# Weight loads issued at two points of an iteration behind a VectorE write, and a later spread of global values

## Chip, cores and metric

The kernel runs on one core of one Trainium2 chip. The metric is device time in microseconds (us) for one execution, the median of several; the profile is one execution recorded by the hardware. TensorE does the matmuls and transposes, VectorE and ScalarE the elementwise work on its results, GpSimd copies inside SBUF, and SyncE issues nearly all transfers from HBM. Each engine works through its own list of instructions in order; they meet at semaphores.

## What is computed

Three layers in float32 on 2176 tokens of width 512 (4 batches, 8 heads of 64; 32 global and 512 local tokens per batch).

```
# attention: global tokens see all; local ones the global tokens and neighbours within 32
out_g = softmax(q_g @ [k_g, k_l].T / 8) @ [v_g, v_l]
out_l = softmax([q_l @ k_g.T, where(|i-j| <= 32, q_l @ k_l.T, -1e9)] / 8) @ [v_g, v_l]
x = concat(out_g, out_l) as (2176, 512)
# soft mixture: 8 experts with 4 slots each
logits = x @ phi
slot_in = softmax(logits, over tokens).T @ x
slot_out[e] = relu(slot_in[e] @ w1[e]) @ w2[e]      # 512 -> 1024 -> 512
x = softmax(logits, over slots) @ slot_out
# feed-forward
h = x @ w_in                                        # 512 -> 2048
out = (h - tanh(h)) @ w_out                         # 2048 -> 512
```

## The kernel before

The order of all work is written out by hand: what the Python code emits first stands first in the list of its engine. The part that matters here is the attention loop, `for it in range(NG + 1)` at line 664, with NG = 32: eight stages `s` (a batch and a half of its heads each) of four iterations `t`.

Iteration `it` does, on TensorE and in this order: the scores of group `it` (`local_scores`, line 248, in two halves `h2`, each followed on VectorE by masked maxima, line 254, and on ScalarE by the exponentials), the transposes of the probabilities of `it-1` (line 269), the product with values of `it-2` (`local_values`, line 281, and `global_values`, line 475), then pieces of other work: scores of the global tokens (line 430), transposes of finished rows (line 311), logits and sums of the mixture (lines 344, 392).

GpSimd prepares operands, all through the helper at line 210. `spread_q(it+1)` copies the queries of the next iteration into the layout that its scores read. `roll_k(it)` and `roll_v(it-2)` shift keys and values by a window. `spread_k(s+1)`, once a stage at t = 1, copies the global keys from the block `qg` into the key tile. `spread_v(s+1)`, once a stage at t = 3, copies the global values of `v[96:128, 0]` into the groups 1 to 5 of the same rows, so that every window's product also covers the global tokens. `local_values` of stage `s` begins in iteration 4s+2.

SyncE issues the loads, in the order in which the code emits them, all through `load` (line 98), which also adds their KB to `queued`. Per stage: queries every second iteration (256 KB, `load_q`), values at t = 2 and t = 3 (`load_v`), `qg` and keys of stage s+2 at the end of t = 3 (`load_qk`, 96 and 576 KB). Between them the loop at line 724 issues weights of later layers: one slot of 512 KB after another (`load_w`, or `load_raw` for the 64-bit words of `w_in`, two transfers of 256 KB), until `queued` reaches a target or slots run out:

```
while queued < LEAD + PACE * it:      # LEAD, PACE = 2700, 1200
```

There are 29 slots. A slot that has not been used has no earlier reader, so its load waits for nothing but its turn on SyncE. Raw words are converted during the loop (`win_head` on ScalarE, `win_ops` on VectorE), and their slots come back. What holds SyncE are the loads whose targets are still read: the queries wait for `spread_q`, `qg` and keys for the global and local scores.

After the loop (about 130 us) come the mixture, lines 971 and 1010, and from about 185 us the feed-forward with lines 1133 and 1174 to 1176.

Of the kernel before, what the change touches and what calls it, by code (L numbers as in the profile page):

```python
# [8 lines left out]
F32 = mybir.dt.float32  # L9
# [8 lines left out]
NST = 8  # L18
NT = 17
NE = 8  # L20
WARM = 3
LEAD, PACE = 2700, 1200
KEEP = 2
SPK = 1
C0 = 4
NIN = 8
# [36 lines left out]
def band_attention_soft_moe_tanhshrink_kernel(  # L63
# [15 lines left out]
    V, S, G, T, DMA = nc.vector, nc.scalar, nc.gpsimd, nc.tensor, nc.sync  # L79
# [47 lines left out]
    def spread_v(s):  # L127
        v = v_t[s][96:128]
        pcopy(v[:, 1:6], v[:, 0:1].to_broadcast([32, 5, 260]))
# [106 lines left out]
    def local_scores(g, fill):  # L236
        s, t = divmod(g, 4)
        k = k_t[s]
        sm = wk.tile([128, 512], F32, tag="sm", name="sm").rearrange("p (j c) -> p j c", j=4)
        mb = wk.tile([128, 4], F32, tag="mb", name="mb")  # L240
        for f in fill[0:1]:
            f()
        for h2 in range(2):
            sc = psS.tile([128, 2, 128], F32, tag="S", name="sc", padded_shape=[128, 2, 256])
            for a in range(2):
                jj = 2 * h2 + a
                for i in range(2):
                    T.matmul(  # L248
                        sc[64 * i:64 * i + 64, a, :], lhsT=q_b[2][:, 256 * i + jj:256 * i + 256:4],
                        rhs=k[:, i, :, WINDOWS[t][jj][0]], skip_group_check=True, tile_position=(0, 64 * i),  # L250
                    )
            for a in range(2):
                jj = 2 * h2 + a
                V.tensor_tensor_reduce(  # L254
                    out=sm[:, jj, :], in0=sc[:, a, :], in1=mask[WINDOWS[t][jj][1]],
                    scale=-0.125, scalar=3e38, op0=ALU.add, op1=ALU.min, accum_out=mb[:, jj:jj + 1],
                )
                S.activation(  # L258
                    out=sm[:, jj, :], in_=sm[:, jj, :], func=AF.Exp, scale=-1.0, bias=mb[:, jj:jj + 1]
                )  # L260
            for f in fill[1 + h2:2 + h2]:
                f()
        sm_t[g] = sm

    def local_transpose(g):
# [239 lines left out]
    free = [(wA, f"w{i}", 1024, 1) for i in range(NSLOT)]  # L505


    def slot(rounded=False):
        kinds = [tuple] if rounded else [(bass.AP, tuple)] if len(w_sl) < len(wq) else [bass.AP, tuple]
        if not any(isinstance(f, k) for k in kinds for f in free):  # L510
            free.extend(cool)
            cool.clear()
        src = free.pop(next(i for k in kinds for i, f in enumerate(free) if isinstance(f, k)))
        if not isinstance(src, tuple):
            return src, src
        pool, tag, width, bufs = src
        return pool.tile([128, width], F32, tag=tag, name="slot", bufs=bufs)[:, 0:1024], src


    def f64_words(src, room=None):  # L520
# [100 lines left out]
    def load_raw():  # L621
        c = len(raw_t)
        raw_t.append(f64_words(wind[:, c, :]))
# [16 lines left out]
    with tc.manual_schedule():  # L640
# [20 lines left out]
        load_v(1, 1)  # L661
        load(out=phi, in_=phid[0])
        fill = []
        for it in range(NG + 1):
            s, t = divmod(it, 4)
            open_chains()
# [42 lines left out]
                spread_k(s + 1)  # L709
            if it == 0:  # L710
                spread_v(0)
            if it < NG and t == 3 and s < NST - 1:
                spread_v(s + 1)
            if it % 2 == 0 and it < NG - 4:
                load_q(it // 2 + 2)
            if it < NG:
# [4 lines left out]
                if t in (2, 3) and 1 <= s < NST - 1:  # L721
                    load_v(s + 1, t - 2)

            while queued < LEAD + PACE * it:
                if len(raw_t) < min(NIN, (it - C0 + 3) // 2 + 1) and free:
                    load_raw()
                elif not len(free) > (KEEP if len(raw_t) < NIN else 0) or not load_w():
                    break
            if it < NG and t == 3 and s + 2 < NST:
                load_qk(s + 2)  # L730
            if it == NG - 5 or it == NG - 1:
# [772 lines left out]
```

## Time and profile before

| what | value |
|---|---|
| three timed runs | 403.26, 405.3, 407.09 us; median 405.3 |
| profiled execution | 406.85 us, of which the span from first to last instruction is 405.1 |
| TensorE clock granted | 0.993 of full speed over the span |
| TensorE matmul busy | 382.9 us, 95% |
| VectorE, ScalarE, GpSimd busy | 276.2, 218.2, 209.7 us |
| read from HBM | 65.22 MB, of 70.43 MB moved |

A stretch's busy time of one engine says how much of it the engine worked; the rest is idle time, and the views of waits say what ended it. The profile calls TensorE's matmuls PE and its loading of the stationary operand PEld, VectorE DVE, ScalarE ACT, GpSimd POOL, and the issuing part of SyncE SPq. "issue" as the cause of a wait means that the profile shows no releaser. A transfer has two times: when SyncE issued it, and how long after that it landed.

### The profile page before, as it was taken

To read this page: it belongs to the slowest core of one execution; us is meant where nothing else is said; L and a number is where in the kernel's file an instruction comes from. 1 tells how busy PE (TensorE), PEld (TensorE's weight loads), DVE (VectorE), ACT (ScalarE), POOL (GpSimd) and SP (SyncE) were. 2 spreads that over 40 slices of the span, in tenths; PEclk is the share of its full clock that TensorE was granted. 3 is DMA by queue.
4 is the path that set the end of the run, shared out by engine and by line. 5 is a ranking of instruction groups with operands and counts; after the bars stand their busy time and mean duration, and the time that the engine had idled before them with its cause. 6 is when DMAs were issued, how large, how long until landed. Compare 5 with 4: busy or idle time off the path is not lost.

```text
span 405.1 us, 10230 instructions
## 1 busy us (share of the span) xinstructions
PE 382.9 (95%) x3767; PEld 279.6 (69%) x3767; DVE 276.2 (68%) x833; ACT 218.2 (54%) x542; POOL 209.7 (52%) x275
## 2 busy tenths in 40 slices
PE   7889889989999899999999999999989999999994
PEld 3677667766787433336877786786868888888873
DVE  4577698766476526449998886787879997555541
ACT  2677666865766202248655645566575645345330
POOL 3676576665564010016866444455575668347441
PEclk9999999999999999999999999999999999999998
DMA  6899999999768989999303101003100003002104
GB/s 182 264 401 317 321 335 268 357 334 294 266 183 270 332 254 418 416 420 385 111 0 105 53 1 53 0 4 94 60 2 2 0 28 129 0 2 113 44 2 138
DMA packets 33834, 70.43 MB, mean 174 GB/s; under 512 B 3824, under 2 KB 10736, under 8 KB 33776
## 3 DMA queue, kind: packets, MB, share of 16 engines
q1 hardware_dynamic: 33632, 69.56, 50.3%
q8 instruction: 32, 0.52, 0.5%
q14 instruction: 26, 0.21, 0.2%
q10 hardware_dynamic: 144, 0.13, 0.1%
HBM read 65.22 MB, written 4.46 MB: 172 GB/s over the span
## 4 chain that ended last, share of the span: by engine, by line
PE 76%; issue 6%; POOL 5%; DVE 4%; DMA 3%; ACT 3%; SPq 2%; DVEq 0%; POOLq 0%
PE a L1175 13%; PE a L1176 13%; PE a L1174 13%; PE sc L248 7%; PE a L971 4%; PE a L1010 4%; PE h L1133 4%; PE X L281 3%; PE ptp L269 3%; SPq L104 2%; PE gsc L430 2%; POOL q L210 2%; PE xTp L311 2%; PE ps L344 1%; DVE slot L1150 1%
## 5 line engine op out<-in xcount | busy, mean ns | idle before, releaser
L1161 POOL TENSOR_TENSOR slot<-slot 128x384 fp32r<-128x384 f32 x96 | 98.7, 1031 | 83.5 <-ACT slot L1157 79.8
L1174 PE MATMUL a<-slot 128*128 128x512 f32 x272 | 106.9, 393 | 1.3 <-ACT v_w L1182 0.7
L1176 PE MATMUL a<-slot 128*128 128x512 f32 x272 | 107.8, 396 | 0.0
L1175 PE MATMUL a<-slot 128*128 128x512 f32 x272 | 107.5, 395 | 0.0
L1146 DVE SCALAR_TENSOR_TENSOR h<-slot,h 128x384 f32<-128x384 f32 x96 | 51.5, 537 | 38.7 <-ACT slot L1140 38.4
L1157 ACT CAST slot<-slot 128x384 fp32r<-128x384 f32 x96 | 47.6, 496 | 49.5 <-DVE slot L1150 49.0
L1140 ACT ACTIVATE slot<-h 128x384 f32<-128x384 f32 x96 | 45.3, 473 | 34.5 <-PE h L1133 33.9
L1174 PEld LDWEIGHTS a<-slot 128*128 128x128 f32 x272 | 51.1, 188 | 14.2 <-ACT v_w L1182 1.5
L1176 PEld LDWEIGHTS a<-slot 128*128 128x128 f32 x272 | 51.0, 188 | 11.4
L1175 PEld LDWEIGHTS a<-slot 128*128 128x128 f32 x272 | 51.0, 188 | 9.3 <-POOL slot L1037 1.0
L1150 DVE TENSOR_TENSOR slot<-slot,h 128x384 f32<-128x384 f32 x96 | 50.8, 529 | 8.0 <-DVE h L1146 0.5
L258 ACT ACTIVATE sm<-sm,mb 128x128 f32<-128x128 f32 x128 | 41.2, 396 | 15.5 <-DVE mb L254 15.2
L248 PE MATMUL sc<-k,q 128*64 128x128 f32 x512 | 39.0, 294 | 4.9 <-POOL q L210 3.8
L210 POOL TENSOR_SCALAR v<-v 32x1300 f32<-32x1300 f32 (+5 forms) x40 | 34.2, 855 | 13.9 <-PE xgp L475 11.4
L248 PEld LDWEIGHTS sc<-k,q 128*64 128x64 f32 x512 | 33.3, 208 | 11.1 <-POOL q L210 5.9
L210 POOL TENSOR_SCALAR q<-q 64x256 f32<-64x256 f32 x62 | 27.5, 444 | 20.5 <-issue 11.0
L254 DVE CUSTOM_DVE_ANT_0 sm<-sc,mask 128x128 f32<-128x128 f32 x128 | 30.2, 284 | 10.9 <-PE sc L248 9.7
L1037 POOL TENSOR_TENSOR slot<-k_w,slot 128x512 fp32r<-128x512 f32 x16 | 20.7, 1296 | 32.5 <-ACT slot L1036 32.3
L1133 PE MATMUL h<-slot 128*128 128x384 f32 x96 | 32.4, 339 | 0.8 <-DVE slot L1150 0.6
L1133 PEld LDWEIGHTS h<-slot 128*128 128x128 f32 x96 | 17.9, 188 | 12.0 <-DVE slot L1150 5.9
L281 PE MATMUL X<-v,pt 128*32 128x65 f32 x1024 | 22.1, 223 | 1.4 <-issue 1.4
L281 PEld LDWEIGHTS X<-v,pt 128*32 128x32 f32 x1024 | 16.5, 109 | 7.2 <-issue 6.1
(239 smaller groups left out, 526.2 us busy)
## 6 DMA issues: line engine op xcount, KB each, us to landing
slot<-in_w_dram SPq DMA_DIRECT2D x55, 512.0 KB, 7.6
slot<-in_w_out_dram SPq DMA_DIRECT2D x9, 512.0 KB, 4.8
slot<-in_w_in_dram SPq DMA_DIRECT2D x16, 256.0 KB, 6.5
k<-in_k_dram SPq DMA_DIRECT2D x7, 576.0 KB, 7.8
q<-in_q_dram SPq DMA_DIRECT2D x15, 256.0 KB, 5.4
out_dram<-o SPq DMA_DIRECT2D x15, 256.0 KB, 2.1
slot<-in_w_in_dram SPq DMA_DIRECT2D x7, 512.0 KB, 10.0
v<-in_v_dram SPq DMA_DIRECT2D x8, 390.0 KB, 5.5
```

What stands on the lines that cost most here:

```text
L210: G.tensor_scalar(out=o, in0=i, scalar1=0.0, scalar2=1.0, op0=ALU.add, op1=ALU.mult)
L248: T.matmul(sc[64 * i:64 * i + 64, a, :], lhsT=q_b[2][:, 256 * i + jj:256 * i + 256:4], rhs=k[:, i, :, WINDOWS[t][jj][0]], skip_group_check ...
L281: T.matmul(X[32 * jj:32 * jj + 32, h, :], lhsT=pt[:, 128 * jj + 32 * h:128 * jj + 32 * h + 32], rhs=v[:, WINDOWS[t][jj][0], 65 * h:65 * h ...
L1133: T.matmul(h, lhsT=mst(128 * fc, 128), rhs=cst(128 * t0 + c.start, n))
L1140: S.activation(out=u, in_=h, func=AF.Square)
L1146: V.scalar_tensor_tensor(out=h, in0=u, scalar=-2.5, in1=h, op0=ALU.add, op1=ALU.mult)
L1150: V.tensor_tensor(out=g, in0=u, in1=h, op=ALU.mult)
L1157: S.copy(out=ghi, in_=g)
L1161: G.tensor_tensor(out=glo, in0=g, in1=ghi.bitcast(F32), op=ALU.subtract)
L1174: T.matmul(acc_t[j], lhsT=ghi[:, c], rhs=whi[fc], start=first, stop=False)
L1175: T.matmul(acc_t[j], lhsT=ghi[:, c], rhs=wlo[fc], start=False, stop=False)
L1176: T.matmul(acc_t[j], lhsT=glo[:, c], rhs=whi[fc], start=False, stop=last)
```

## The change

The body of the loop at line 724 becomes a function `load_ahead(it, to)`. It is called at the end of an iteration, as before, and for iterations 2 to 26 also in the middle of `local_scores`, after VectorE's masked maxima of the first half, with half an iteration less in the target. LEAD grows from 2700 to 3300. In these iterations the first slot taken in each call is written by VectorE, one element, before its load is issued, so that the load waits for VectorE to have come to that point of its list; later loads stand behind it on SyncE. The spread of global values of stage `s` (from the second stage on) is emitted at the end of iteration 4s+1 instead of 4s-1; at t = 1 it follows `spread_k` on GpSimd.

```
-LEAD, PACE = 2700, 1200
+LEAD, PACE = 3300, 1200
@@ local_scores, at the end of each half h2
+            if h2 == 0 and 2 <= g < NG - 5:
+                load_ahead(g, g - 0.5)
@@ slot
-        return pool.tile([128, width], F32, tag=tag, name="slot", bufs=bufs)[:, 0:1024], src
+        t = pool.tile([128, width], F32, tag=tag, name="slot", bufs=bufs)[:, 0:1024]
+        if beat:
+            beat.pop()
+            V.memset(t[0:1, 0:1], 0.0)
+        return t, src
@@ ahead of the loop
+        def load_ahead(it, to):
+            beat[:] = [1] * (2 <= it < NG - 5)
+            while queued < LEAD + PACE * to:
+                if len(raw_t) < min(NIN, (it - C0 + 3) // 2 + 1) and free:
+                    load_raw()
+                elif not len(free) > (KEEP if len(raw_t) < NIN else 0) or not load_w():
+                    break
+            beat.clear()
@@ in the loop
-            if it < NG and t == 3 and s < NST - 1:
-                spread_v(s + 1)
+            if it < NG and t == 1 and s:
+                spread_v(s)
...
-            while queued < LEAD + PACE * it:
-                if len(raw_t) < min(NIN, (it - C0 + 3) // 2 + 1) and free:
-                    load_raw()
-                elif not len(free) > (KEEP if len(raw_t) < NIN else 0) or not load_w():
-                    break
+            load_ahead(it, it)
```

## Rows read from the trace of the kernel before

**Rows 1.** The page's head: span, and busy time of TensorE.

```profile
span 405.1 us, 10230 instructions
...
PE 382.9 (95%) x3767; PEld 279.6 (69%) x3767; DVE 276.2 (68%) x833; ACT 218.2 (54%) x542; POOL 209.7 (52%) x275
```

**Rows 2.** Stretches: length, busy us (instructions) per engine, TensorE clock, DMA share, GB/s.

```profile
10.00:50.00 40.00, 35.44 (x715) 28.06 (x719) 26.40 (x140) 28.05 (x77) 26.37 (x49) 1.00 0.97 325
50.00:90.00 40.00, 36.61 (x805) 28.77 (x804) 31.97 (x154) 27.75 (x83) 28.47 (x49) 1.00 0.99 321
90.00:130.00 40.00, 38.16 (x840) 30.04 (x841) 24.56 (x139) 26.89 (x77) 22.08 (x44) 1.00 0.79 255
...
20.00:30.00 10.00, 8.91 (x215) 7.18 (x206) 7.30 (x41) 7.89 (x24) 7.68 (x16) 1.00 1.06 400
```

**Rows 3.** Waits, 0 to 140 us: who for whom, us in total, times, longest.

```profile
PE sc L248 <- POOL q L210: 3.8, 8, 1.0
...
POOL k L210 <- DMA qg<-in_qg_dram: 4.4, 4, 2.2
```

**Rows 4.** TensorE's time line (start, length, work [idle before]): gaps without releaser.

```profile
20.83 0.32 PE L475 MATMUL xgp<-v,pg 128*32 128x65 f32 x7 [0.30 <-issue]
...
86.53 0.86 PE L344 MATMUL ps<-xT,phi 128*32 128x128 f32 x23 [1.38 <-issue]
...
106.31 0.33 PE L460 MATMUL gtp<-ident,pg 128*128 128x128 f32 x1 [0.69 <-issue]
```

**Rows 5.** SyncE's time line, and that transfer's KB and us to landing.

```profile
21.31 0.54 SPq L104 DMA_DIRECT2D qg<-in_qg_dram  x1
...
qg<-in_qg_dram SPq DMA_DIRECT2D x1, 96.0 KB, 7.2
```

**Rows 6.** GpSimd's time line, and (last) all `spread_v` grouped: busy, mean ns.

```profile
20.69 2.45 POOL L210 TENSOR_SCALAR v<-v 32x260 f32<-32x260 f32 x3 [0.45 <-PE xgp L475]
...
28.68 0.51 POOL L210 TENSOR_SCALAR k<-qg 128x384 f32<-128x384 f32 x1 [1.08 <-DMA qg<-in_qg_dram]
...
29.47 0.88 POOL L210 TENSOR_SCALAR q<-q 64x256 f32<-64x256 f32 x2
...
42.98 0.75 POOL L210 TENSOR_SCALAR k<-qg 128x384 f32<-128x384 f32 x1 [0.69 <-DMA qg<-in_qg_dram]
...
74.34 1.05 POOL L210 TENSOR_SCALAR k<-qg 128x384 f32<-128x384 f32 x1 [0.39 <-DMA qg<-in_qg_dram]
...
L210 POOL TENSOR_SCALAR v<-v 32x1300 f32<-32x1300 f32 x8 | 10.9, 1359 | 0.8 <-DMA v<-in_v_dram 0.2
```

**Rows 7.** VectorE: its last work of iteration 3, and its smallest memsets, grouped.

```profile
21.60 0.28 DVE L486 TENSOR_SCALAR gx<-xgp,grs 128x64 f32<-128x64 f32 x1
...
L185 DVE MEMSET mask<- 128x32 f32 x2 | 0.2, 85 | 0.0
```

**Rows 8.** TensorE's time line: scores (L248) and values (L281) around the spreads.

```profile
13.76 1.23 PE L248 MATMUL sc<-k,q 128*64 128x128 f32 x16 [1.00 <-POOL q L210]
...
24.52 1.23 PE L248 MATMUL sc<-k,q 128*64 128x128 f32 x16 [0.44 <-POOL q L210]
...
27.66 1.23 PE L248 MATMUL sc<-k,q 128*64 128x128 f32 x16 [0.35 <-POOL q L210]
...
29.40 0.67 PE L281 MATMUL X<-v,pt 128*32 128x65 f32 x32
...
31.54 1.18 PE L248 MATMUL sc<-k,q 128*64 128x128 f32 x16
...
39.20 1.23 PE L248 MATMUL sc<-k,q 128*64 128x128 f32 x16 [0.29 <-POOL q L210]
...
44.10 0.67 PE L281 MATMUL X<-v,pt 128*32 128x65 f32 x32
...
70.73 1.23 PE L248 MATMUL sc<-k,q 128*64 128x128 f32 x16 [0.39 <-POOL q L210]
...
75.75 0.67 PE L281 MATMUL X<-v,pt 128*32 128x65 f32 x32
```

More of the change, by code (lines that the diff above doesn't have):

```diff
@@ L505, in band_attention_soft_moe_tanhshrink_kernel @@
     free = [(wA, f"w{i}", 1024, 1) for i in range(NSLOT)]
+    beat = []
     def slot(rounded=False):
```

## The prediction

> **What bounds the kernel now.** I read the page's summary, busy time by stretch, the waits of TensorE and GpSimd, and then the time lines of both around the spreads. TensorE is busy for 382.9 us of the 405.1 us span [rows 1]: a change can win only what TensorE stands idle in the stage that the change touches. The edits act in the attention loop (33 iterations, to about 130 us); what follows starts with the same weights loaded, because the slots run out before the loop ends in either version (29 slots, the last filled in iteration 25 before, 24 after, by the loop's own arithmetic). In that loop TensorE is idle for 4.56, 3.39 and 1.84 us in three stretches of 40 us [rows 2], 9.8 us in all. So the ceiling of any gain is about 9.8 us, 2.4%.
>
> That idle time has two causes that the trace names. One is GpSimd, which copies the next queries (`spread_q`): eight waits, 3.8 us [rows 3]; the longest, 1.00 us at 13.76 [rows 8], stands in iteration 2, ahead of what the edits reach. The other has no releaser: seven gaps inside runs of matmuls, from 0.30 to 1.38 us; the first, the longest and the last are shown [rows 4], and the other four are 0.51, 1.17, 0.67 and 0.90 us, 5.6 us in all.
>
> The DMA engines are the second thing to look at: share 0.97 and 0.99 with 325 and 321 GB/s in the first two stretches, 0.79 only in the third [rows 2]. They are full from 10 to 90 us. A transfer then lands when the bytes ahead of it are through: the q/k block of stage 2 (`qg`, 96 KB) was issued at 21.31 us and landed 7.2 us later, at 28.5 [rows 5], because 512 KB slots stood ahead. GpSimd waited for such blocks in four places, 4.4 us [rows 3]; three of them are in the loop, where `spread_k` starts at 28.68, 42.98 and 74.34 after 1.08, 0.69 and 0.39 us of idle [rows 6].
>
> **The change, part by part.**
>
> *Level of weights.* The loop stops loading when the bytes queued reach a target. Before, the end of iteration `it` filled to 2700+1200it; after, it fills to 3300+1200it, and the middle to 2700+1200it. Counting through the code, with KB of page section 6, `qg` of stage 2 has 6738 KB ahead of it before and 7250 after; stage 3 11611 and 12123; stage 5 20845 and 21357. That is one slot, 512 KB, more each time. The queries and values loaded at even iterations get 512 to 1536 KB more ahead. In a full queue 512 KB are 1.3 us at 400 GB/s (20 to 30 us) and 1.6 us at 325 [rows 2]. The queue must be full for this: at 22.6 us, when SyncE would issue `qg`, 21.9 us being the end of VectorE's work of iteration 3 [rows 7] and one slot's issue lying between, the landing at 29.8 (28.5+1.3) is still 7.2 us off, the latency that this row had. So the hold doesn't set the landing; the queue does.
>
> *The hold.* 30 loads carry a one-element memset, 17 in the middle and 13 at the end of an iteration. The nearest row is a memset of 32 columns, 85 ns [rows 7]: 2.6 us of VectorE over 25 iterations, 0.1 us in each. VectorE is busy 26 to 32 of 40 us [rows 2], so I take 0 for the path; with no cover it would be 2.6. Behind a held load in SyncE's order wait the queries (every second iteration), values and `k`. The queries wait for `spread_q` of the same iteration anyway, which comes after the scores of both halves, while the middle memset stands behind the first half: 0. `qg` and `k` are held to the end of iteration 4s+3, but by the paragraph above the queue is later than the hold: 0, if the queue stays full.
>
> *The spread of values.* `spread_v` (32x1300, 1.36 us mean [rows 6]) leaves the end of iterations 4s+3. There it stood ahead of the next `spread_q`: with two short rolls it is the 2.45 us at 20.69 [rows 6], and the scores of iteration 5 waited 0.44 us at 24.52, those of 9 0.29 at 39.20, those of 17 0.39 at 70.73 [rows 8]. These three waits go. It comes to the end of iteration 4s+1, behind `spread_k`, which waits for `qg`. Its reader is close: `local_values(4s)` in iteration 4s+2 reads rows 96 to 128 of four groups, which `spread_v` writes. Before, it had two iterations of slack; now it has the time of one scores group and one transpose: 1.74 us from 27.66 to 29.40 [rows 8].
>
> *Stage 1 (iterations 5, 6).* `qg` lands at 29.8; `spread_k` starts 0.17 us after the landing as before, 29.97; 0.51 us for it [rows 6], 1.36 for `spread_v`, 0.05 to release: values can start at 31.9. TensorE started them at 29.40 [rows 8]. **+2.5 us**; the 0.44 us won at iteration 5 is spent inside this wait. The first scores after it, at 31.54 [rows 8], move along.
>
> *Stage 2 (9, 10).* `spread_k` from 42.98+1.6 = 44.6, takes 0.5 to 0.75, `spread_v` 1.36: values at 46.6, with the release. TensorE would be there at 44.10 [rows 8] + 2.5 - 0.29 = 46.3. **+0.3, -0.29**: the delay is there already and most of it is not paid twice, since the transfers run on while TensorE waits.
>
> *Stage 4 (17, 18).* 74.34+1.6 = 75.95; this `spread_k` took 1.05 [rows 6], more often 0.5; with 1.36 values start at 77.9 to 78.4. TensorE would be there at 75.75 [rows 8] + 2.5 - 0.39, and with stage 2 level at 77.9. **+0.3, -0.39.**
>
> *Other stages.* There `spread_k` did not wait for a transfer. GpSimd's own chain is 0.51+1.36 = 1.87 us after `spread_q`, TensorE's 1.74: at most 0.13 each; I take 0. The following `spread_q` moves behind by 1.4 us; in stage 1 it ended at 30.35 (29.47 and 0.88 [rows 6]), 1.2 us before the scores that need it, at 31.54 [rows 8], and these scores move by 2.5. I take the same slack for the other stages: 0, and 0.2 each without it.
>
> *A rule beside the rows.* Of the seven gaps without a releaser the rows show only length and place [rows 4]. The Trainium skill, "Runtime: NRT & Kernel Launch", section "Instruction fetch mechanics", says that each sequencer drives its own DMA queue to refill instructions in 16 KiB blocks and that this is mostly hidden. No row here ties the gaps to it. By that rule the gaps owe nothing to the queue of weights and stay: the sum is +2.4. If instead the gaps were refills held up by data, a smoother queue could take back up to their 5.6 us, and the sum would be -3.2.
>
> **The sum.** 2.5 + 0.3 - 0.29 + 0.3 - 0.39 = +2.4 us. The profiled execution took 406.85 us (span 405.1), so it would be 409.3. The three timed runs had a median of 405.3, 1.55 us under the profiled one; the same +2.4 gives **407.7 us**.
>
> Bounds. If the extra 512 KB delay nothing, `spread_k` starts at 28.68 as before and values at 30.6: +1.2 in stage 1, nothing in stage 2, 0.1 in stage 4, and with the two waits won +0.6. If the queue is later by 1536 KB (the largest push of any load) instead of 512, 2.6 us come on top, and with an uncovered memset 2.6 more: +7.6.
>
> **Rivals.**
> 1. *Each stage pays* (slower by over 1%). The hold lets the DMA queue run dry; then `qg` lands a fixed time after VectorE's end of iteration 4s+3, and a late TensorE no longer gives the transfers time to catch up. Each of the three waiting stages then pays about stage 1's 2.5 less its own gain: 7.5 - 0.7 = +6.8, 412.1 us. For it: the queue is nearly empty already where the share is 0.79 [rows 2]. Against: 325 GB/s at share 0.97 leaves no room to run dry before 90 us, and later no `spread_k` waited. It decides from about 2 us of empty queue ahead of each `qg`.
> 2. *The smoother queue pays* (faster by over 1%). The gaps without a releaser shrink because weights no longer come in bursts, and `qg` lands no later. Then 5.6 us and 0.7 us of waits come back, less 1.2 us of stage 1: -5.1, 400.2 us. For it: in the third stretch, with share 0.79, TensorE idles 1.84 us instead of 4.56 and 3.39 [rows 2]. Against: the last gap, 0.69 us at 106.31, lies in that stretch [rows 4], and the level of weights rises rather than falls.
> 3. *Nothing of it shows.* `qg` lands as before, the end of `spread_k` plus 1.36 meets TensorE a little late in stage 1 and two or three waits of `spread_q` go: +0.6 by the lower bound, 405.9 us. It differs from the forecast only in whether 512 KB more delay `qg`; for it speaks that every microsecond TensorE stands gives the queue as much time, against it the full queue of 20 to 30 us [rows 2].
>
> **How the numbers follow.** Forecast (+1.2 to +4) 0.42; nothing shows (-1.5 to +1.2) 0.22; each stage pays, or the later queue of the upper bound, (+4 to +8) 0.24; the smoother queue pays (below -1.5) 0.12, a third of it within 1%. One per cent is 4.05 us, about what a measurement of this kernel can tell from no change: three runs lie 3.8 us apart. Faster by over 1%: 0.08. Slower by over 1%: 0.24. Within: 0.68. The predicted time is 407.7. The range leaves out the worst tenth at both ends: 402.5 (-2.8) below, between the smoother queue and no effect, and 411.5 (+6.2) above, short of the full price of rival 1. The forecast's own range is 406.5 to 409.3.
>
> **What would show it.** In the profile after: `spread_k` of stage 1 starts near 30 us instead of 28.68, `spread_v` comes right behind it, and the values matmul of iteration 6 waits about 2.5 us for GpSimd, the largest such wait in the loop; the same matmul in iterations 10 and 18 waits under 1 us. The scores of iterations 5, 9 and 17 no longer wait for `spread_q`. SyncE's waits on GpSimd give way to waits on VectorE. The rest of the program, from the end of the loop, keeps its length. Wrong would be: a landing of `qg` that follows the hold and not the bytes ahead; gaps without a releaser that are fewer by more than 2 us; a wait of ScalarE for raw weights, which land up to 1.6 us later than before.

## The result, and the profile after

The changed kernel took a median of 410.63 us (four runs, 409.89 to 412.01), the kernel before 406.19 us (four runs, 403.26 to 407.32). The ratio is 1.014, with a 95% interval of 1.0093 to 1.0188: slower by 1.4%, about 5.7 us; the two medians lie 4.4 us, 1.1%, apart. The profiled execution took 410.43 us, its span 408.6 us. A second set of runs on another occasion gave 1.0124 [1.0068, 1.0179]. The forecast was +2.4 us, 0.6%, to 407.7 us: the right sign, and by the ratio less than half of the size. The measured time lies inside the stated range (402.5 to 411.5) and outside the forecast's own (406.5 to 409.3).

The first view is TensorE's waits from 0 to 140 us of the kernel after (who waited for whom; us in total, times, longest), which answers [rows 3].

```profile
PE X L283 <- POOL v L210: 4.1, 4, 2.4
PE sc L248 <- POOL q L210: 2.6, 4, 1.0
```

A wait that did not exist before is now the largest: the values matmul (L281 before, L283 now) waits for `spread_v`. The wait for queries fell from 3.8 to 2.6 us. GpSimd's waits for the q/k block were 4.4 us [rows 3] and are 7.2 here, but that shows no effect of the change: a second execution of the kernel before has 7.2 us as well. First the kernel after, then that execution:

```profile
POOL k L210 <- DMA qg<-in_qg_dram: 7.2, 5, 2.6
...
POOL k L210 <- DMA qg<-in_qg_dram: 7.2, 5, 2.4
```

The busy time by stretch, with the columns of [rows 2] (length, busy us per engine, TensorE clock, DMA share, GB/s):

```profile
10.00:50.00 40.00, 33.70 (x689) 26.67 (x689) 24.64 (x143) 27.18 (x75) 26.36 (x49) 1.00 0.99 328
50.00:90.00 40.00, 36.36 (x774) 28.58 (x770) 30.46 (x160) 27.57 (x76) 25.61 (x44) 1.00 0.96 295
90.00:130.00 40.00, 37.94 (x831) 30.02 (x829) 24.90 (x150) 26.06 (x78) 22.89 (x45) 1.00 0.82 256
```

TensorE's busy time in the first stretch fell by 1.7 us, in the others by 0.2 each. The time lines around stage 1 answer [rows 5], [rows 6] and [rows 8] (start, length, work, idle before and its releaser). SyncE first, then VectorE's hold write, GpSimd and TensorE, all of the kernel after:

```profile
21.25 2.11 SPq L104 DMA_DIRECT2D slot<-in_w_dram  x2
23.46 0.55 SPq L104 DMA_DIRECT2D qg<-in_qg_dram  x1
...
22.72 0.06 DVE L524 MEMSET slot<- 1x1 f32 x1
...
30.55 0.51 POOL L210 TENSOR_SCALAR k<-qg 128x384 f32<-128x384 f32 x1 [2.56 <-DMA qg<-in_qg_dram]
31.14 1.27 POOL L210 TENSOR_SCALAR v<-v 32x1300 f32<-32x1300 f32 x1
...
32.47 0.60 PE L283 MATMUL X<-v,pt 128*32 128x65 f32 x27 [2.38 <-POOL v L210]
47.24 0.61 PE L283 MATMUL X<-v,pt 128*32 128x65 f32 x27 [0.87 <-POOL v L210]
...
63.35 0.60 PE L283 MATMUL X<-v,pt 128*32 128x65 f32 x27 [0.40 <-POOL v L210]
...
95.42 0.55 PE L283 MATMUL X<-v,pt 128*32 128x65 f32 x24 [0.48 <-POOL v L210]
```

The block was issued at 23.46 instead of 21.31 us, `spread_k` started at 30.55 instead of 28.68, `spread_v` came right behind it, and the values of iteration 6 waited 2.38 us. The two times of the block differ as much between executions of one kernel: in the second one of the kernel before it was issued at 23.15 us and `spread_k` started at 30.85. What is new is that the values stand behind `spread_k`. Three later stages (2, 3 and 5) pay a wait of the same kind, 1.75 us together.

The rest of the program kept its length: from the first matmul that reads mixture weights to the end of the span it is 264.6 us before (405.1 - 140.47) and 265.1 after (408.6 - 143.49). So everything lies in the loop. The table below adds up, for eight executions, TensorE's idle time by what ended it, from 11 us to that first mixture matmul, and the time lost to a lower granted clock in that part (one minus the granted clock, summed by 1 us stretches). The kernels named in the last four columns come with the experiments. All are in us.

| | before | before, again | after | after, again | move alone | no hold | no hold, again | hold at one point |
|---|---|---|---|---|---|---|---|---|
| first mixture matmul at | 140.47 | 139.13 | 143.49 | 146.52 | 138.97 | 141.62 | 141.13 | 150.73 |
| values wait for `spread_v` | 0 | 0 | 4.13 | 5.47 | 3.98 | 3.62 | 3.45 | 13.52 |
| scores wait for queries | 3.20 | 3.44 | 1.59 | 1.55 | 1.61 | 1.59 | 1.62 | 1.60 |
| gaps without releaser | 5.62 | 2.37 | 4.75 | 4.17 | 0 | 1.69 | 2.11 | 0.67 |
| lost to lower clock | 0 | 0.85 | 0 | 3.81 | 0.57 | 1.98 | 2.86 | 3.41 |

In each column the first line less the sum of the other four is 131.1 to 133.0 us, so these four lines carry the differences, but up to 1.9 us between two columns stay unexplained. Between the means of the two executions before and the two after, the loop grew by 5.2 us: +4.8 from values, -1.75 from queries, +0.5 from gaps, +1.5 from the clock, together 5.0. That is in line with the timed 4.4 to 5.7 us. What the change did by waits that the trace names is thus about +3 us, and about 2 us came in two lines that the prediction gave no price. Of the 3.81 us of lower clock 3.4 lie behind two waits inside the loop, in one execution of the two; the rest, like the 0.85 of the kernel before, lies at the loop's very end.

### The profile page after: what moved, and what is told of

It is laid out like the page before. It is cut to its first block, busy times and chain, and to the rows that moved or that the text cites. A ratio compares the mean times of both kernels' runs of the same rounds, so it can differ in the third digit from the quotient of the medians.

```text
span 408.6 us, 10285 instructions
## 1 busy us (share of the span) xinstructions
PE 383.6 (94%) x3767; PEld 280.3 (69%) x3767; DVE 275.5 (67%) x863; ACT 218.8 (54%) x542; POOL 209.1 (51%) x275
## 5 line engine op out<-in xcount | busy, mean ns | idle before, releaser
L248 PE MATMUL sc<-k,q 128*64 128x128 f32 x512 | 39.0, 294 | 3.6 <-POOL q L210 2.6
L248 PEld LDWEIGHTS sc<-k,q 128*64 128x64 f32 x512 | 33.3, 208 | 9.4 <-issue 5.0
L283 PE MATMUL X<-v,pt 128*32 128x65 f32 x1024 | 23.7, 223 | 5.8 <-POOL v L210 4.1
L283 PEld LDWEIGHTS X<-v,pt 128*32 128x32 f32 x1024 | 17.2, 109 | 12.5 <-issue 6.4
```

Of the source, the lines that this page charges most:

```text
L248: T.matmul(sc[64 * i:64 * i + 64, a, :], lhsT=q_b[2][:, 256 * i + jj:256 * i + 256:4], rhs=k[:, i, :, WINDOWS[t][jj][0]], skip_group_check ...
```

## The experiments

The theories at the start: (a) the forecast's, that the extra 512 KB ahead of `qg` and the late `spread_v` make the cost, and the hold none; (b) that the hold itself delays `qg` in every stage (rival 1); (c) that the new place of `spread_v` makes it, whatever the loads do. Later came (d), that the gaps without a releaser are refills of instructions held up behind the transfers. In the expectations theory A stands for (a), C and H for (b), B for (c) and G for (d). Ratios are to the kernel before, with a 95% interval.

### How far two runs of one kernel agree

Both kernels were run again, without an edit. The kernel before:

> The kernel before, unchanged, as a run of its own: how far two sets of runs of one program differ, and a second trace of it. Every theory: ratio 1.000 with an interval that holds 1. Theory G (the gaps without a releaser lie at fixed places of TensorE's list and differ from run to run): gaps at some of the seven places of the first trace and at others, their sum anywhere from 0 to 6 us, with the loop's length following it. Against G: the same seven gaps with the same lengths.

Measured: 405.7 us, 0.9986 [0.9947, 1.0025]. The kernel after:

> The changed kernel again, beside the other runs of this group: ratio 1.008 to 1.015 if its loss is the late spread (4.1 us of waits of the values matmul, 1.2 us of waits for queries won back, about +3 us) and some chance in the gaps; 1.006 to 1.008 if the gaps of the first set were only chance. Its trace: the values matmul of iteration 6 waits 2.0 to 2.8 us for GpSimd again; the gaps without a releaser need not be where they were.

Measured: 411.58 us, 1.0124 [1.0068, 1.0179]. The change's cost is repeated. The kernel before had two gaps instead of seven, as theory G has it. The profiled spans are 404.5 us beside 405.1, and 411.7 beside 408.6. What differs between the two executions of the kernel after is in the table: 3.81 us of lower clock in one and none in the other.

### Hold and second point, each with and without the other

Four kernels have the late `spread_v`; they differ in whether the loop loads at one point (LEAD 2700, as before) or at two (LEAD 3300), and whether loads are held. The move alone, one point and no hold, on the kernel before:

```
-            if it < NG and t == 3 and s < NST - 1:
-                spread_v(s + 1)
+            if it < NG and t == 1 and s:
+                spread_v(s)
```

> The kernel before with one edit: the global values of stage s are spread at the end of iteration 4s+1 instead of 4s-1; weights as before. Theory A (a fuller queue delays qg, and the late qg now stands ahead of the spread that the values matmul waits for): qg lands as before, near 28.5 us, so the values matmul of iteration 6 starts near 30.6 instead of 29.40 (+1.2 us), and the three waits of the scores behind a spread_v go (-0.7): +0.3 to +1.2 us, ratio 1.001 to 1.003. Theory B (the spread in its new place costs about as much without the weights, because GpSimd is the bound at t = 1): a wait of over 2 us in iteration 6 here too, +3 us or more, ratio 1.008 or more.

Measured: 407.04 us, 1.0033 [0.9958, 1.0108]. Values now wait in six stages, 0.23 to 1.18 us each, 3.98 us in all, and the queries' wait halves. The wait of iteration 6 is 0.82 us, not the 2 us and more of theory B. So the move by itself already takes the slack that [rows 8] showed, in each stage and not only in the first; this execution had no gap without a releaser at all, which is why its loop is not longer.

Two points without the hold, on the kernel after (run twice):

```
-            beat[:] = [1] * (2 <= it < NG - 5)
+            beat[:] = []
```

> The changed kernel without the memsets: weights at two points with LEAD 3300, issued as soon as SyncE comes to them; the spread stays at 4s+1. Theory A (bytes ahead in a full queue set the landing of qg, not the hold): qg of stage 2 lands at 30 to 30.5 us as in the changed kernel, values of iteration 6 wait about 2.4 us: ratio to before 1.010 to 1.016. Theory C (the hold makes the queue run dry and holds qg back on SyncE): qg lands 1 us or more earlier, the wait of iteration 6 halves, ratio 1.000 to 1.007.

> The changed kernel without the memsets once more, with more rounds: two points, LEAD 3300, spread at 4s+1. If the hold costs by itself: ratio 1.000 to 1.006, clear of the changed kernel's 1.012 to 1.014. If the hold is free, as the prediction said: 1.008 to 1.014.

Measured: 407.44 us, 1.004 [0.9967, 1.0113], and 409.37 us, 1.0073 [1.0031, 1.0115]. The second lies between the two ranges that were expected. The wait of iteration 6 did not halve, as theory C had it: it was 2.99 and 2.38 us. One point with the hold, on the kernel after:

```
-LEAD, PACE = 3300, 1200
+LEAD, PACE = 2700, 1200
@@ local_scores
-            if h2 == 0 and 2 <= g < NG - 5:
-                load_ahead(g, g - 0.5)
```

> The changed kernel with LEAD 2700 and without the point in the middle: weights at the end of an iteration as before, but held there until VectorE's write; spread at 4s+1. It differs from the kernel that only moves the spread (ratio 1.003) by the hold alone. Theory A (the place of the spread and the bytes ahead of qg are all): same as that kernel, ratio 1.001 to 1.006, gaps without a releaser anywhere from 0 to 6 us. Theory H (the hold costs by itself: it spreads the weights over the time, TensorE's gaps without a releaser grow, and qg and keys wait on SyncE behind it): ratio 1.008 to 1.014, gaps 4 us or more.

Measured: 417.36 us, 1.0273 [1.0211, 1.0335], the slowest of all, twice the cost that theory H expected, and with 0.67 us of gaps instead of the 4 and more that it expected. So the four are:

| | no hold | hold |
|---|---|---|
| loads at one point | 1.0033 | 1.0273 |
| loads at two points | 1.004, 1.0073 | 1.014, 1.0124 |

At one point the hold alone costs 2.4%, 9.7 us of 406; the forecast had it at nothing. At two points it costs the difference of the means, 1.0132 - 1.0057 = 0.0075, about 3 us, with some 0.0055 to either side if the intervals are taken as independent: clear of nothing, but only just. The mean without the hold, +0.57% or 2.3 us, is what the forecast's sum gave: it had priced a kernel without the hold. That the two agree so well is in part luck. In the table, the two executions without the hold have +3.5 us of values, -1.7 of queries, -2.1 of gaps and +2.0 of lower clock against the two before, and the last two were in no sum.

Where the hold bites, the time lines of GpSimd and SyncE show; first the move alone, the `spread_k` of stages 1 to 3 and the issue of the block that stage 2 reads:

```profile
28.94 0.51 POOL L210 TENSOR_SCALAR k<-qg 128x384 f32<-128x384 f32 x1 [1.64 <-DMA q<-in_q_dram]
44.03 0.51 POOL L210 TENSOR_SCALAR k<-qg 128x384 f32<-128x384 f32 x1 [1.38 <-DMA k<-in_k_dram]
59.34 0.62 POOL L210 TENSOR_SCALAR k<-qg 128x384 f32<-128x384 f32 x1 [0.82 <-DMA k<-in_k_dram]
...
37.39 0.63 SPq L104 DMA_DIRECT2D qg<-in_qg_dram  x1
```

Its first two stretches of 40 us:

```profile
10.00:50.00 40.00, 35.30 (x705) 27.96 (x706) 25.65 (x138) 27.42 (x75) 26.42 (x49) 1.00 0.93 313
50.00:90.00 40.00, 37.81 (x822) 30.10 (x822) 31.40 (x162) 29.44 (x86) 27.27 (x49) 1.00 0.98 329
```

Then the same of the kernel with the hold at one point, behind SyncE's largest wait up to 140 us. The kernels without a hold have no such wait for VectorE:

```profile
SPq L104 <- DVE mb L254: 25.0, 8, 4.6
```

```profile
30.66 0.51 POOL L210 TENSOR_SCALAR k<-qg 128x384 f32<-128x384 f32 x1 [3.94 <-DMA qg<-in_qg_dram]
48.11 0.51 POOL L210 TENSOR_SCALAR k<-qg 128x384 f32<-128x384 f32 x1 [2.19 <-DMA k<-in_k_dram]
66.75 0.51 POOL L210 TENSOR_SCALAR k<-qg 128x384 f32<-128x384 f32 x1 [2.67 <-DMA k<-in_k_dram]
...
41.15 0.06 DVE L522 MEMSET slot<- 1x1 f32 x1
41.24 0.89 SPq L104 DMA_DIRECT2D slot<-in_w_in_dram  x2
42.83 0.54 SPq L104 DMA_DIRECT2D qg<-in_qg_dram  x1
```

Its stretches:

```profile
10.00:50.00 40.00, 32.31 (x609) 25.41 (x609) 23.76 (x135) 26.53 (x74) 23.74 (x44) 0.96 0.90 285
50.00:90.00 40.00, 35.09 (x712) 27.52 (x712) 25.90 (x136) 23.27 (x64) 22.57 (x41) 0.96 0.88 277
```

SyncE stands behind VectorE's work for 25 us, up to 4.6 at a time: its load issued at 36.16 us is followed by the held one at 41.24, right behind the hold write at 41.15. The block that stage 2's `spread_k` reads is issued at 42.83 us instead of 37.39 and starts `spread_k` 5.3 us later (48.11), where without the hold it took 6.6 us (44.03). Some of these rows name a load of keys or queries as the releaser; `qg` itself had landed 0.1 to 0.2 us before each of these starts (at 28.8, 43.9 and 59.2 us in the move alone, 30.5, 47.9 and 66.6 with the hold). Less is moved: 285 and 277 GB/s instead of 313 and 329. From stage 2's `spread_k` on, the block lands 4.0 to 5.4 us after its issue, and every stage waits: six waits of values, 1.27 to 3.76 us.

With two points the same shows weakly. Counted from the values matmul of iteration 6, the block that stage 2's `spread_k` reads was issued 7.8 and 9.4 us later in the two executions of the kernel after, 5.4 and 5.9 us in the two without the hold, 6.5 in the move alone and 10.3 with the hold at one point. It landed 12.7 and 13.8 us after that matmul with the hold, 12.3 in both without. From 50 to 90 us the kernel after moved 295 and 297 GB/s, the one without the hold 319 and 313. Without the hold, `spread_k` waits in stage 1 and stage 5 only (lines of the first run: six spreads, stages 1, 2 and 5 shown):

```profile
31.37 0.51 POOL L210 TENSOR_SCALAR k<-qg 128x384 f32<-128x384 f32 x1 [3.38 <-DMA k<-in_k_dram]
46.68 0.51 POOL L210 TENSOR_SCALAR k<-qg 128x384 f32<-128x384 f32 x1
...
91.16 0.51 POOL L210 TENSOR_SCALAR k<-qg 128x384 f32<-128x384 f32 x1 [0.39 <-DMA qg<-in_qg_dram]
```

The kernel after waits there for 1.07 us in stage 2 and 0.97 in stage 5:

```profile
45.33 0.51 POOL L210 TENSOR_SCALAR k<-qg 128x384 f32<-128x384 f32 x1 [1.07 <-DMA qg<-in_qg_dram]
...
93.50 0.51 POOL L210 TENSOR_SCALAR k<-qg 128x384 f32<-128x384 f32 x1 [0.97 <-DMA qg<-in_qg_dram]
```

In stage 1 the wait is there without the hold too (3.38 us), so there the hold sets nothing, as forecast. From stage 2 on it does. In the table of the result, the hold's 3 us at two points are +1.3 in values (4.8 against 3.5), +2.6 in gaps without releaser and -0.5 in clock. Only the first is tied to the hold by the traces; the last two are not shown to belong to it: see the gaps below.

### One slot fewer ahead

```
-LEAD, PACE = 3300, 1200
+LEAD, PACE = 2700, 1200
```

> The changed kernel with LEAD 2700: two points, held, spread at 4s+1, but the target at the end of an iteration is that of the kernel before and the one in the middle 600 KB under it. Theory A (bytes ahead of qg): 512 KB fewer ahead of it, qg of stage 2 lands near 28.7 to 29.2 us instead of 30.4, the values matmul of iteration 6 waits 0.8 to 1.4 us instead of 2.4: 1.5 us under the changed kernel, ratio to before 1.003 to 1.007. Theory C (the hold on SyncE makes qg late): no gain, qg near 30 us, ratio as the changed kernel.

Measured: 410.81 us, 1.012 [1.0067, 1.0173], no gain over the kernel after. `spread_k` of stage 1 started at 29.57 instead of 30.55, and the values' wait there was 2.03 us instead of 2.38 and 2.66; stage 2 paid 1.14 instead of 0.87 and 0.74. So the 512 KB ahead move stage 1 in the direction of (a), by about 0.5 us of TensorE's wait, given back in stage 2, and not by the 1.3 us worked out in the prediction; the move of `spread_k` is within what two executions of one kernel differ by (28.68 and 30.85 before). The time tells that one slot of level does not carry the cost.

### The q/k block ahead of the held loads

```
-            load_ahead(it, it)
             if it < NG and t == 3 and s + 2 < NST:
                 load_qk(s + 2)
+            load_ahead(it, it)
```

> The changed kernel with one swap on SyncE: at the end of iteration 4s+3, qg and keys of stage s+2 are issued ahead of the held weights. Theory A: 512 KB fewer ahead of qg, in stage 2 landing near 29 us, the wait of iteration 6 1.0 us instead of 2.4; ratio to before 1.003 to 1.007. Theory C: qg no longer stands behind the hold, so it is issued 1 to 2 us earlier in every stage; where the queue is short it lands that much earlier and the waits of iterations 10, 14 and 22 (0.87, 0.40, 0.48 us) go too: ratio 0.998 to 1.003.

Measured: 407.34 us, 1.005 [1.0015, 1.0084]. The values' waits fall to three, 0.92 us in all, from 4.13 and 5.47:

```profile
30.50 0.60 PE L283 MATMUL X<-v,pt 128*32 128x65 f32 x27 [0.20 <-POOL v L210]
...
46.88 0.60 PE L283 MATMUL X<-v,pt 128*32 128x65 f32 x27 [0.50 <-POOL v L210]
...
61.77 0.61 PE L283 MATMUL X<-v,pt 128*32 128x65 f32 x27 [0.22 <-POOL v L210]
```

With the hold still in place, its cost through `qg` goes when `qg` no longer stands behind held loads. That is (b)'s mechanism, though the ratio lies in the range expected by A (1.003 to 1.007) and not by C. The edit covers the bytes ahead of `qg` at the end of the iteration as well, so this run alone does not divide the two theories; the four kernels above do.

### The order of the spreads

In the kernel after, values ahead of `spread_k`:

```
+            if it < NG and t == 1 and s:
+                spread_v(s)
             if it < NG and t == SPK and s < NST - 1:
                 spread_k(s + 1)
...
-            if it < NG and t == 1 and s:
-                spread_v(s)
```

> The changed kernel with one swap: at the end of iteration 4s+1 the spread of global values stands ahead of the spread of global keys, so that it no longer waits for qg. Theory A: the values matmuls of iterations 6, 10, 18 wait no more; the late qg delays only the queries of iteration 7 (about 32.3 us against scores wanted at 31.1, so about 1 us once): 2 to 3 us under the changed kernel, ratio to before 1.003 to 1.009. Theory B (the spread costs in whatever order, because GpSimd has 1.3 us more at t = 1): same as the changed kernel, 1.011 to 1.017.

Measured: 407.65 us, 1.0038 [0.9961, 1.0115]. No value waits for GpSimd any more. The chain is thus the one forecast: the late block delays `spread_k`, and through GpSimd's order `spread_v` and the values. In the kernel after, `spread_v` back at its old place, an iteration and a half earlier:

```
-            if it < NG and t == 1 and s:
-                spread_v(s)
+            if it < NG and t == 3 and s < NST - 1:
+                spread_v(s + 1)
```

> The changed kernel with the spread of global values put back to the end of iteration 4s-1; weights at two points, held, LEAD 3300. Theory A: qg is as late as in the changed kernel (30.4 us), but no values matmul waits behind it; instead the spread of iterations 7, 11, 15 ... waits for global values that stand behind 1024 to 1536 KB more and land 3 to 4.5 us later than before, and the scores of iterations 9, 13, 17 wait for the queries behind that spread, 1 to 3 us each at first: +3 to +6 us, ratio 1.007 to 1.015, the same or worse than the changed kernel. Theory B (the spread's place is the cost, the weights are harmless): within 1 us of before, ratio 0.998 to 1.003.

Measured: 415.84 us, 1.0164 [1.0054, 1.0273]. Here the scores wait for queries, which stand behind `spread_v` on GpSimd:

```profile
41.95 1.23 PE L248 MATMUL sc<-k,q 128*64 128x128 f32 x16 [2.80 <-POOL q L210]
...
58.98 1.23 PE L248 MATMUL sc<-k,q 128*64 128x128 f32 x16 [1.26 <-POOL q L210]
...
75.22 1.23 PE L248 MATMUL sc<-k,q 128*64 128x128 f32 x16 [1.70 <-POOL q L210]
```

With the old place the loads cost no less by the ratio, 1.0164 against 1.014 and 1.0124, in a wide interval. So moving the spread is not by itself what made the change slow, but its place behind `spread_k` is one way in which the late block reaches TensorE.

### Is there a version that gains?

Three kernels put the better orders together: the kernel before with values first at t = 1; that with `load_qk` ahead of the weights as well; and the kernel after with both edits (the two edits are those shown above).

> The kernel before with the spread of global values at the end of 4s+1, ahead of the spread of global keys; weights as before. Theory A: no values matmul waits for GpSimd, the three waits of the scores behind the spread (1.1 us) go, the queries of iterations 7, 11 ... come 1.3 us later and find slack: 0 to -1.5 us, ratio 0.996 to 1.000.

Measured: 406.02 us, 1.0 [0.9968, 1.0032].

> The kernel before with the spread of values at 4s+1 ahead of that of keys, and qg and keys of stage s+2 issued ahead of the weights at the end of 4s+3; no hold. Theory A: besides what the kernel without the second edit wins, the three waits of the spread of keys for qg (2.2 us on GpSimd) go; they lie off TensorE's path for the most part: ratio 0.995 to 0.999. It would be the fastest version if the theory holds.

Measured: 408.71 us, 1.0038 [0.9998, 1.0077].

> The changed kernel with the hold, but the spread of values ahead of that of keys, and qg and keys issued ahead of the held weights: no values matmul waits for GpSimd. If the hold costs only by standing ahead of qg: ratio 0.997 to 1.002, as the same edits without the hold. If it costs through the gaps too: 1.004 to 1.008, gaps of 4 us or more in its trace.

Measured: 409.11 us, 1.0055 [1.0016, 1.0093]. None beats the kernel before. In the first, values wait for nothing and the queries' wait is 1.99 us instead of 3.20 and 3.44; the 1.3 us do not show in the time. The second missed its expected gain. The third lies in the range that was expected for a hold that costs through the gaps, and has the gaps for it, 7.14 us; but the second, without the hold, has 6.36. The second and third differ in hold and second point, and their intervals lie over each other: once `qg` stands ahead and values come first, what is left of the hold can't be told from nothing.

### The gaps without a releaser

These lie at few places of TensorE's list, but their length differs from run to run: in the kernel before 5.62 us in one execution and 2.37 in another. One place, ahead of transposes at L454 (`gtp`; L452 in the kernel before), had a gap in nine of the eighteen executions traced, of 0.67 to 2.30 us, and none in the others. In the kernel after, run again, it was the longest:

```profile
59.02 0.55 PE L454 MATMUL gtp<-ident,pg 128*128 128x128 f32 x3 [2.30 <-issue]
```

The view of DMA queues shows a packet of 16 KB on an instruction queue between 56.0 and 56.6 us of that execution (packets, MB, share of 16 engines), 2.4 to 3 us before the gap's end, and transfers of data filling the engines then:

```profile
q1 hardware_dynamic: 62, 0.14, 97.6%
q8 instruction: 1, 0.02, 14.5%
```

In the kernel before, all seven gaps [rows 4] end 2.3 to 2.8 us after the start of such a packet. Over the eighteen traces the same holds for all 80 gaps from 11 to 131 us, at 2.2 to 2.9 us; but of some 320 such packets three in four are followed by no gap. So the gaps go with refills of instructions, and theory (d) would say why some refills cost time: they come late behind data. To test it, the kernel before with no mixture weights issued before iteration 16 and two a call from there:

```
-            while queued < LEAD + PACE * it:
+            room_w = 0 if it < 16 else 2 if it < NG - 5 else 99
+            while True:
                 if len(raw_t) < min(NIN, (it - C0 + 3) // 2 + 1) and free:
                     load_raw()
-                elif not len(free) > (KEEP if len(raw_t) < NIN else 0) or not load_w():
+                elif room_w and len(free) > (KEEP if len(raw_t) < NIN else 0) and load_w():
+                    room_w -= 1
+                else:
                     break
```

> The kernel before with no slot of the mixture's weights loaded ahead of iteration 16, and two an iteration from there on; raw words, queries, keys, values as before. Only the first half of the loop is to be read. Theory G (the gaps without a releaser come from the transfers that fill the DMA engines): with the share near 0.6 in iterations 4 to 15, no gap over 0.3 us there, where the first trace had 0.51, 1.17 and 0.67; qg of stages 2 and 3 lands within 4 us, and no spread waits for it. If the gaps have nothing to do with transfers: gaps of the same kind there, 1.5 us or more in all.

Measured, a single execution: 411.85 us. Its first stretch, and of its five gaps from 10 to 130 us the first and the last:

```profile
10.00:50.00 40.00, 37.34 (x767) 29.03 (x763) 28.48 (x147) 29.23 (x83) 27.67 (x50) 0.99 0.67 205
```

```profile
85.31 0.86 PE L344 MATMUL ps<-xT,phi 128*32 128x128 f32 x23 [1.65 <-issue]
...
120.60 1.01 PE L344 MATMUL ps<-xT,phi 128*32 128x128 f32 x10 [2.67 <-issue]
```

With a DMA share of 0.67 there TensorE has no such gap up to 80 us; once the weights come, five gaps make 7.0 us. TensorE was busy 37.34 us in the first stretch, against 35.44 before [rows 2]. That agrees with (d) but does not show it. With full queues the move alone had no gap at all, the kernel before, run again, had none from 22.3 to 104.7 us, and the kernel with values first was busy for 37.31 us of that stretch at a share of 0.95. `qg` of stages 2 and 3 landed 4.8 and 5.2 us after its issue, not within the 4 expected; no spread waited for it up to 80 us. A milder form, PACE 1000 instead of 1200, was tried on the kernel before and on the one with values first:

```
-LEAD, PACE = 2700, 1200
+LEAD, PACE = 2700, 1000
```

> The kernel before with PACE 1000 instead of 1200: the slots are full near iteration 30 instead of 25, the DMA engines have a sixth less to do per iteration until then. Theory G (gaps without a releaser are refills behind full queues): gaps under 1.5 us in all, spread of keys waits for qg nowhere, loop 2 to 3 us shorter: ratio 0.991 to 0.997, unless the mixture then waits for weights (up to 2 us, lines 971 and 1010). If the gaps are independent of the load: 0.998 to 1.002.

Measured: 406.37 us, 1.0011 [0.9978, 1.0044].

> As the kernel with PACE 1000, and the spread of values at 4s+1 ahead of that of keys: 0.5 to 1 us fewer waits for queries besides: ratio 0.988 to 0.996 by theory G, 0.997 to 1.001 if gaps don't depend on the load.

Measured: 406.18 us, 1.002 [0.999, 1.0051]. The gain that (d) promised did not come: the gaps stayed at 3.58 and 3.22 us, between the two executions of the kernel before. In the first, `spread_k` waited for `qg` nowhere in the loop, as expected, and the DMA share was still 0.92 and 0.86 in the first two stretches. Whether the queue was still too full for the refills or the gaps do not depend on it, these runs do not tell. Theory (d) stays open.

Whether the hold lengthens the gaps stays open. In the seven executions with two points and the hold they are 3.53 to 7.14 us, 4.9 on average; in the nine without it (the late weights left out) 0 to 6.36, 3.0 on average. With the hold at one point they are 0.67. The ranges lie over each other, and the one execution without gaps (the move alone) shows how far chance goes.

## Why the prediction was wrong, point by point

- **What bounds the kernel, and the ceiling**: right. All that changed lies in the loop; what follows kept its length within 0.8 us in all four executions of the two kernels.
- **Level of weights**: half right. `qg` of stage 2 was issued at 23.46 us, not 22.6, and `spread_k` started at 30.55, not 29.97. But one slot fewer moved it by 1.0 us and TensorE's wait by 0.35 to 0.6, not the 1.3 to 1.6 of the working, and brought no time; and the kernel before, run again, has the block later (30.85) than the kernel after. A likely reason, not shown, is that what TensorE loses the transfers gain, which the prediction applied to stages 2 and 4 but not to its own 1.3.
- **The hold: this step failed.** It was priced at nothing with the words "the hold doesn't set the landing; the queue does". With two points that held for stage 1, the one stage from which it was worked out, and not from stage 2 on; with one point it held nowhere (values of iteration 6 wait 3.76 us with the hold and 0.82 without). The hold alone costs 9.7 us at one point and about 3 us at two, of which the traces tie 1.3 to waits of values. The latency of 7.2 us in [rows 5] was read as the queue's, and the condition "if the queue stays full" was taken as met, because the share was 0.97 and 0.99. But the full queue was made by loads that nothing held; with the hold the same share cannot be assumed. In the kernel after, `qg` lands 4.7 to 5.3 us after its issue in four of the five later stages, and 4.4 to 5.3 in three of five in its second execution (6.9 to 8.5 before): by these landings the queue ahead of it is shorter, and a later issue is a later landing.
- **Memsets**: right. Each takes 0.06 us, 1.8 us of VectorE in 30; apart from the loads that they hold, one 0.2 us wait of a weight load of TensorE is all that is put down to them in the kernel after. VectorE's busy time, read as 26 to 32 of 40 us, is 24.6 to 32 [rows 2].
- **Stage 1**: right, 2.38 and 2.66 us where +2.5 was forecast, values at 32.47 where 31.9 was; the move alone has 0.82 where the working had 1.2. The largest wait of the loop is where it was put.
- **Other stages**: too low. Stages 2, 4 and the rest were +0.3, +0.3 and 0. Measured were 0.87, 0 and, in stages 3 and 5, 0.40 and 0.48; in the second execution 0.74, 0.29, and 0.24 and 1.54. The prediction gave these stages GpSimd's bare chain, 1.87 us against TensorE's 1.74. But where the chain has no slack, every lateness of `spread_k` passes to the values, also one that was harmless before: the move alone waits in all six stages.
- **The queries**: right in kind. The waits of iterations 5, 9 and 17 are gone: -1.75 us where -1.12 was forecast.
- **SyncE**: as said, waits for GpSimd give way to waits for VectorE:

```profile
SPq L104 <- DVE mb L254: 22.0, 14, 2.3
SPq L104 <- POOL q L210: 17.1, 11, 5.2
SPq L104 <- DVE slot L524: 13.7, 10, 2.7
```

  where the kernel before waited 41.3 us for GpSimd's queries. The third row is the hold write itself.
- **Rival 1** was the mechanism that was missing, in a mild form. Its sum, 412.1 us, is the nearest to the 410.63 measured; its point of decision, 2 us of empty queue ahead of each `qg`, was not measured. The nearest figures are SyncE's longest waits for VectorE's maxima, 2.3 us in the kernel after and 4.6 with the hold at one point.
- **Rival 2 and the rule of the Trainium skill**: the gaps did not shrink. The Trainium skill, "Runtime: NRT & Kernel Launch", section "Instruction fetch mechanics", says that refills come in 16 KiB blocks and that crossing a block is mostly hidden. The 16 KB packets ahead of the gaps agree with the first. With the second the traces agree for three packets in four; behind the others TensorE stands for up to 2.30 us, and 2.67 in the kernel with late weights.
- **Not priced at all**: what a stall brings after it. The last section has it; in the mean of two executions it is 1.5 us of the 5.2, all of it from one of them.
- **The signs of being wrong**: the first came, a landing of `qg` that follows the hold, from stage 2 on. The other two did not: the gaps are not fewer by 2 us, and ScalarE waits for no raw weights.

## What to carry to other kernels

Price a new wait on a load by the issue time of every transfer queued behind it, in each stage, not by whether the queue is full in the trace of before: the full queue may be the work of the very loads that are now held. Put small transfers that a critical chain needs ahead of the held bulk ones (1.005 instead of 1.013), and test a combined change in its four combinations, which here divided in one table what no single run could. A step that is moved to stand just ahead of its reader hands on every lateness of what stands before it: count its slack in each stage.

## What the hardware showed that was not expected

**A stall can be followed by a lower clock.** In the second execution of the kernel after, TensorE waited 2.66 us before 32.28 and 2.30 before 59.02. In the stretches just behind each, the granted clock is 0.51 and 0.56, for the most part the level of 1.2 GHz:

```profile
32.50:35.50 3.00, 3.00 (x66) 1.80 (x56) 0.77 (x3) 0.00 (x0) 1.98 (x4) 0.51 1.03 393
59.50:62.50 3.00, 3.00 (x47) 2.62 (x48) 0.61 (x3) 1.20 (x4) 0.24 (x1) 0.56 1.02 306
```

In the first execution the same wait was 2.38 us, and the same stretch stands at 2.4 GHz:

```profile
32.50:35.50 3.00, 3.00 (x90) 2.39 (x90) 1.59 (x5) 0.00 (x0) 2.16 (x4) 1.00 1.01 382
```

TensorE is busy for the whole 3 us in both, but the records hold 66 matmuls instead of 90. By the granted clock each such stretch cost 1.7 us, and the one of the kernel with late weights, at a wait of 2.67 us, cost 3.4. Over the executions of this study it came with waits of 1.21, 1.43, 1.76, 1.99, 2.06, 2.30, 2.38, 2.66, 2.67, 2.99 and 3.76 us, and not with others of 2.03, 2.17, 2.38, 2.50 and 2.80; so the wait's length alone does not decide, and what does stays open here.

**A latency measured in a full queue is no property of the transfer.** The same 96 KB took 6.9 to 8.5 us from issue to landing in all six stages before (6.5 to 8.6 in the second execution), and 4.7 to 5.3 us in four of the five later stages of the kernel after; in stage 1 it was 7.2 and 6.9. In the kernel with late weights, whose first stretch had a share of 0.67, it took 4.7 to 5.2 us up to 70 us and 8.5 and 8.6 once the weights came.
